# A DeltaNet recurrence feeding a hard-swish MLP on one core: the keys' transposes behind the products with the state, two steps with joined runs of small matmuls, and one last store per queue

## The chip, the cores and the metric

The kernel runs on one core of one Trainium2 chip. The metric is the device time of one execution in microseconds (us). Engines by the profile's names: PE is TensorE's matmuls, PEld its weight loads, DVE VectorE, ACT ScalarE, POOL GpSimd, SP SyncE, which only issues DMAs.

## The reference

The first half is a linear recurrence with a state matrix for each of 4 batches and 8 heads, over 768 tokens with head dimension 48. The second half is an MLP over the 3072 tokens by 384 features that the first half gives.

```
k_n = k / (norm(k) + 1e-6)
for t in range(768):                        # per batch and head
    y[t]  = q[t] @ state                    # 48 x 48 state, 0 at the start
    v_old = state^T k_n[t]
    state = state + beta[t] * outer(k_n[t], v[t] - v_old)
x   = y as (3072, 384)
h   = x @ w_in                              # 384 x 2048
g   = h * clip(h + 3, 0, 6) / 6
out = g @ w_out                             # 2048 x 384
```

All data are float32.

## The kernel before

**Chunks.** The tokens are cut into 24 steps of 32. In one step the 128 partitions hold 4 batches of 32 tokens. The recurrence inside a chunk becomes matrix products: a triangular matrix of the keys' scores per batch and head is inverted, and the state moves on once per step.

**What a step t issues.** `chain(t)` (L776) is the step's own serial work: `ks` (L795), 32 small matmuls of keys and queries with the state; `R` on DVE; `pz` (L816), 32 small matmuls with the inverse; `py` (also L816) with the scores; `su` (L927), the state's update; and `yt` (L862), three transposes of the output, which ACT copies to `xT` (L866), the input of the MLP. `prep(t)` (L494) prepares step t + 6 in five pieces: `kb` on POOL (the keys scaled, L499); four transposes of the keys on TensorE (L513), their copy by ACT (L521) and the mask on POOL (L475); the same transposes for the queries; `sc` (L536), 32 small matmuls that give the scores; and two DVE operations that mask the scores (L547), with the scaled keys on POOL (L487).

**The filler.** The MLP is cut into units that a generator (`mlp_units`, L1286) hands out one at a time between those pieces. Two steps make one block of 256 tokens. For blocks from the third on, the up projection (`up_by_eleven`, L1048) works with 11 products of 128 x 128 in place of 12, and the down projection (`down_by_seven`, L1196) with 7 in place of 8. In the trace up-projection matmuls are `ph` and down-projection ones `po`. From step 8 on, even steps are mostly filled with `ph` units, odd ones with `po` units.

**Small tiles and the full array.** `ks`, `pz`, `py`, `su` and `sc` place each matmul on a part of TensorE's array (`tile_position` or 64 rows), several side by side; a run of 32 shows as 64 loads and 64 matmuls in the trace. `ph`, `po` and the transposes use the full 128 x 128 array.

**The order of work** is written by hand: `ORDER` (L22), a list of words, for steps 0 to 4, and from step 5 on the loop at L1458. There a step has 15 slots `u`. In each slot `plan[u]` issues pieces of `chain` (`ch`) and `prep` (`now`), then one MLP unit follows. `later`, in slot 13, is the first piece (`kb`) of the prep that the next step will go on with. Step 5 (`behind`) has a plan of its own. From step 6 on, the slots around the change are:

```
0: ks            1: R, keys' transposes      2: R, queries' transposes
4: pz, scores    5: masks on the scores      (steps 8 and 12, APART: scores in 6, masks in 7)
```

Every engine works through its own queue in that order. PSUM buffers of the ring `pm` (four) are chosen when the program is written: the one whose last reader was issued first.

**Stores.** Each step's 128 x 384 output is stored by `to_dram` (L1136), one DMA for each batch of 32 rows. `py` leaves the batches in swapped order (`b ^ 1`), which `to_dram` undoes. All stores go out on SP, except that for the last two steps every second one goes out on ACT. The last block's first step is stored in two halves of 192 columns, so the end of the kernel has three stores of four DMAs.

Of the kernel before, what the change touches and what calls it, by code (L numbers as in the profile page):

```python
# [14 lines left out]
ACTF = mybir.ActivationFunctionType  # L15
# [29 lines left out]
def kernel(  # L45
# [21 lines left out]
    nc = tc.nc  # L67
    B, H, S, D = q.shape
    DM, FF = moe_w_in.shape
    C, DP = 32, 64  # L70
    P = B * C
    assert P == 128 and S % C == 0 and D <= DP and H % 2 == 0
    N = S // C
# [6 lines left out]
    CB = 2  # L80
# [14 lines left out]
    def rows(b):  # L95
        return slice(C * b, C * b + C)
# [4 lines left out]
    def group(t):  # L101
        return (0, t) if t < G0 else ((t - G0) // GS + 1, (t - G0) % GS)
# [34 lines left out]
    def needs(*what):  # L137
        assert past.issuperset(what), (what, set(what) - past)
# [5 lines left out]
    def ring(tag, n, key):  # L144

        held = rings.setdefault(tag, [])
        i = len(held)
        if i < n:
            held.append(key)
        else:  # L150
            i = min(range(n), key=lambda i: reads.get(held[i], len(reads)))
            needs(("read", held[i]))
            held[i] = key
        slot[tag] = f"{tag}{i}"

    def read(*keys):
        for key in keys:
            past.add(("read", key))
            reads.setdefault(key, len(reads))
# [49 lines left out]
    for j, value in enumerate((1.0, -1.0)):  # L209
        m = mask2[:, j, :]  # L210
        for b in range(B):
            nc.gpsimd.memset(mask2[rows(b), j, :], value)
            nc.gpsimd.affine_select(
                out=mask2[rows(b), j, :], in_=mask2[rows(b), j, :], pattern=[[1, C]],
# [89 lines left out]
    for i, n in enumerate((0, 1, 2, 3, 4, 5, 0, 1, 3, 4, 5, 0, 1, 5, 0, 1)):  # L304
        s, f = weights[i][0].shape[1:]
# [458 lines left out]
    xTs, outs, zs = {}, {}, {}  # L764
# [5 lines left out]
    def he(h):  # L770
        return (h % 2) * NP + h // 2

    def by_pair(t):
        return t.rearrange("p (a e w) -> p e a w", e=2, w=D)

    def chain(t, whole=True):  # L776
# [29 lines left out]
        def plus(out, ph, sign, into):  # L806
            for e in range(2):
                nc.vector.scalar_tensor_tensor(
                    out=by_pair(out)[:, e], in0=ph[:, e], scalar=sign, in1=by_pair(into)[:, e],
                    op0=ALU.mult, op1=ALU.add,  # L810
                )
# [14 lines left out]
        def output(Z=None):  # L826

            if t > 0:
                needs(("turned", t - 1))
            y = work.tile([P, DM], FP32, name="y", bufs=1)  # L830
            if t > 0:
                nc.scalar.activation(
                    out=by_pair(y[:]), in_=even, func=ACTF.Copy, scale=parity[:, 1, 1:2]
                )
                past.add(("even", t))
                if ("R", t) in past:
                    read(("ks", t, 0))
                yield 1
                plus(y[:], odd, parity[:, 0, 1:2], y[:])
                read(*(("ks", t, i) for i in range(2)))  # L840
                yield
            needs(("Z", t))
            Z = zs.pop(t)
            ring("pm", NPM, ("py", t))
            py = psM.tile([P, 512], FP32, name="py", tag=slot["pm"])
            of_heads(py, lambda b: b ^ 1, lambda h: LB[:, he(h), :], Z)
            past.add(("BZ", t))
            yield
            if t == 0:
                nc.scalar.activation(out=y[:], in_=py[:, 0:DM], func=ACTF.Copy)  # L850
            else:
                nc.vector.tensor_tensor(out=y[:], in0=y[:], in1=py[:, 0:DM], op=ALU.add)
            read(("py", t))
            yield
            blk, cc = divmod(t, CB)
            if cc == 0:
                needs(*([("up", blk - 2)] if blk >= 2 else []))
                xTs[blk] = work.tile([128, NKT, TB], FP32, name="xT")
            ring("pm", NPM, ("yt", t))
            pt = psM.tile([128, NKT, P], FP32, name="yt", tag=slot["pm"])  # L860
            for s in range(NKT):
                nc.tensor.transpose(pt[:, s, :], y[:, s * 128 : (s + 1) * 128], ident[:])  # L862
            past.add(("turned", t))
            yield 1
            read(("yt", t))
            nc.scalar.activation(  # L866
                out=xTs[blk][:, :, cc * P : (cc + 1) * P], in_=pt[:], func=ACTF.Copy
            )
            past.add(("seam", t))
            yield  # L870

# [11 lines left out]
        else:  # L883
# [5 lines left out]
            for e in range(2):  # L889
                nc.vector.scalar_tensor_tensor(  # L890
                    out=Rp[:, e].rearrange("p (a w) -> p a w", w=D), in0=even[:, e],
# [4 lines left out]
            if whole:  # L896
                yield
            nc.vector.scalar_tensor_tensor(
                out=Rp, in0=odd.rearrange("p e a w -> p e (a w)"), scalar=parity[:, 1, 0:1],
# [43 lines left out]
        for i, x in enumerate(su):  # L943
            sv = state[:, 2 * i : 2 * i + 2].rearrange("p b a w -> p b (a w)")
            nc.vector.tensor_tensor(
                out=sv, in0=sv, in1=x[:, :, 0 : NP * D], op=ALU.subtract
# [187 lines left out]
                yield  # L1134

    def to_dram(t, o, m=slice(0, DM)):  # L1136
        for b in range(B):
            r0 = b * S + t * C
            eng = nc.scalar if t >= N - CB and b % 2 else nc.sync
            eng.dma_start(out=out[r0 : r0 + C, m], in_=o[rows(b ^ 1), m])  # L1140

    def down(blk, c, f0):

# [186 lines left out]
    def take(gen, n=1):  # L1330
        for _ in range(n):
            while next(gen, None) == 1:
                pass
# [107 lines left out]
    with tc.manual_schedule():  # L1441
        for word in ORDER.split():
            word, _, n = word.partition("*")
            for _ in range(int(n or 1)):
                do(word)
        for name in relus:
            settle(0, name)
        while evicts:
            evicts.pop(0)()

        units = gens["u"]
        fill = inverse_of(2)
        loads = iter(())
        left = due = 0
        USED = {"up": 0.42, "eleven": 1.0, "down": 0.7}
        APART = (8, 12)
        CHAIN = {0: 0.45, 1: 0.75, 2: 0.75, 3: 0.4, 4: 0.4, 6: 0.5, 9: 0.8, 10: 0.6, 14: 0.2}
        for t in range(LS, N):  # L1458
            g, i = group(t)
            ch = chain_of(t)  # L1460
            behind = t == LS
            now, more, third, later = (prep_of(t + LA - n) for n in (2, 1, 0, -1))
            if not behind:
                now = third
            take(gens["v"], 4)
            if i == 0:
                left += 1
            if i == 2:
                loads = keys_of(g + 3)
            plan = {  # L1470
                0: lambda: take(ch),
                1: lambda: (take(ch), take(now)),
                2: lambda: (take(ch), take(now), take(gens["q"], 4)),
                3: lambda: take(ch),
                4: lambda: (take(ch), take(now, t not in APART)),
                5: lambda: take(now, t not in APART),
                6: lambda: take(now),
                7: lambda: take(now, t in APART),
                8: lambda: take(ch),
                9: lambda: take(ch),  # L1480
                10: lambda: take(ch),
                11: lambda: token_sums(t // CB),
                13: lambda: take(later),
            }
            if behind:
                plan[13] = None
                for u, gen in zip((3, 5, 5, 6, 7, 9, 10, 11, 12, 13), (more,) * 5 + (third,) * 5):
                    plan[u] = lambda old=plan.get(u), gen=gen: (old and old(), take(gen))
            ready = (1, 6)
            for u in range(NU):  # L1490
                if plan.get(u):
                    plan[u]()
                take(loads, 2)
                if (i, u) == (0, 2):
                    drain(fill)
                    left = 0
                    fill = norms_of(g + 2)
                if (i, u) == ready:
                    drain(fill)
                    fill = inverse_of(g + 1)  # L1500
                    take(fill)
                    left, due = 2 * (C - 2) + 2, 0.0
                take(rest)
                take(gens["a"])
                take(units)
                settle(1)
                while evicts:
                    evicts.pop(0)()
                if i == 1 == ready[0] and 5 < u < 7:
                    continue  # L1510
                if i == 0 or not left:
                    take(fill, 2 if i or u < 2 else u > 4)
                    continue
                room = max(1.65 - USED[mode["of"]] - CHAIN.get(u, 0), 0.15) / mode["mean"]
                due += room * left / max((GS - i) * NU - u, 1)
                due = min(due, 2.6)
                take(fill, int(due))
                left, due = max(left - int(due), 0), due - int(due)
            if behind:
                take(later)  # L1520
            drain(ch)
        for _ in units:
            settle(2)
# [30 lines left out]
```

## Time and profile before

| | us |
|---|---|
| median of 3 runs (662.1 to 663.01) | 662.82 |
| the profiled execution | 662.71 |
| its span, first to last instruction | 661.0 |

The span is what the profile covers; the profiled execution's own time is 1.7 us longer. The busy shares, the lengths of single steps and the timelines are shown where the prediction uses them. A timeline row reads: start and length in us, engine, line, operation, output from inputs, shapes, count, and in brackets the idle time before it with what ended it. Starts follow each other more closely than the lengths say, since matmuls are pipelined; a run's pace is read from start to start. A float32 matmul shows as two loads and two matmuls, a transpose as one of each. A row of the windows reads: window, its length, then busy time and count of each engine, clock, share and rate of the DMA. Of the DMA queues, q8 carries TensorE's instructions.

### The profile page before, as it was taken

The numbers are of one execution on the slowest core, as the hardware profiler recorded it, in microseconds if no ns is written. First come the engines' busy times: TensorE is split into PE (matmuls) and PEld (weight loads), VectorE is DVE, ScalarE is ACT, GpSimd is POOL, SyncE is SP. The second block draws the span as 40 slices with busy tenths as digits, with TensorE's granted clock in tenths as the row PEclk, the third lists the DMA queues.
The fourth block names the chain that finished last, engine by engine and source line by source line (L and its number), as shares of the span: only waits on it lengthen the run. The fifth ranks groups of instructions, "written<-read, shape, count | busy, mean of one in ns | idle before, by whom it ended". The sixth has DMA issues, their size and how long they took to land.

```text
span 661.0 us, 26631 instructions
## 1 busy us (share of the span) xinstructions
PE 632.6 (96%) x11640; PEld 568.8 (86%) x11640; DVE 499.5 (76%) x1164; ACT 263.2 (40%) x547; POOL 226.6 (34%) x352
## 2 busy tenths in 40 slices
PE   2768999999999999999999999999999999999997
PEld 2658987776689989999999999999999999999997
DVE  5899877798657988758988748979658998456354
ACT  4786578322232154154144244244244144153240
POOL 5531023003661354453254354164152241331330
PEclk9979999999999999999999999999999999999999
DMA  7888246212041030041030030030020020000101
GB/s 171 210 216 217 76 100 165 49 25 39 16 84 20 2 75 3 3 83 28 3 74 3 2 74 3 2 63 2 3 50 2 2 49 3 23 18 2 26 1 24
DMA packets 88692, 33.28 MB, mean 50 GB/s; under 512 B 80224, under 2 KB 83424, under 8 KB 88576
## 3 DMA queue, kind: packets, MB, share of 16 engines
q1 hardware_dynamic: 88224, 31.29, 21.5%
q8 instruction: 91, 1.49, 0.9%
q10 hardware_dynamic: 352, 0.30, 0.2%
q14 instruction: 25, 0.20, 0.1%
HBM read 26.84 MB, written 4.72 MB: 48 GB/s over the span
## 4 chain that ended last, share of the span: by engine, by line
PE 91%; DVE 3%; DMA 2%; ACT 2%; SPq 1%; issue 1%; ACTq 0%; DVEq 0%
PE po L1215 28%; PE ph L1055 27%; PE ph L983 9%; PE po L1151 6%; PE ks L795 4%; PE pz L816 3%; PE pt L513 3%; PE py L816 3%; PE su L927 3%; PE sc L536 3%; ACT spare L345 1%; PE yt L862 1%; DMA w_out<-in_moe_w_in_dram 1%; SPq L168 1%; PE pi L673 1%
## 5 line engine op out<-in xcount | busy, mean ns | idle before, releaser
L1055 PE MATMUL ph<-xT,w_in 128*128 128x128 f32 (+1 forms) x720 | 156.7, 321 | 0.2 <-issue 0.2
L1019 POOL TENSOR_TENSOR g<-g 128x256 f32<-128x256 f32 (+1 forms) x144 | 88.0, 612 | 105.5 <-ACT g L1069 99.9
L1055 PEld LDWEIGHTS ph<-xT,w_in 128*128 128x128 f32 x720 | 116.9, 191 | 6.7
L1215 PE MATMUL po<-w_out,g 128*128 128x192 f32 x640 | 110.6, 326 | 0.0
L1215 PEld LDWEIGHTS po<-w_out,g 128*128 128x128 f32 x640 | 104.6, 190 | 0.5
L1215 PE MATMUL po<-spare,g 128*128 128x192 f32 x480 | 86.7, 332 | 0.0
L1069 ACT ACTIVATE g<-ph 128x512 f32<-128x512 f32 x72 | 43.0, 597 | 107.5 <-PE ph L1055 107.5
L1215 PEld LDWEIGHTS po<-spare,g 128*128 128x128 f32 x480 | 77.2, 190 | 1.8
L983 PE MATMUL ph<-xT,w_in 128*128 128x128 f32 (+1 forms) x384 | 72.8, 339 | 1.5 <-ACT xT L866 0.6
L1225 POOL TENSOR_TENSOR o<-o,u 128x192 f32<-128x192 f32 x18 | 14.9, 828 | 163.5 <-ACT o L1222 76.1
L983 PEld LDWEIGHTS ph<-xT,w_in 128*128 128x128 f32 x384 | 60.2, 196 | 9.0 <-DVE g L993 0.9
L1082 DVE TENSOR_TENSOR g<-ph,g 128x256 f32<-128x256 f32 x72 | 30.2, 419 | 47.3 <-PE ph L1055 44.8
L748 DVE TENSOR_TENSOR pr<-A 128x30 f32<-128x30 f32 (+9 forms) x150 | 57.6, 384 | 3.3
L1201 DVE TENSOR_TENSOR g<-g 128x512 f32<-128x512 f32 x80 | 55.3, 712 | 3.6 <-PE po L1215 3.6
L1102 DVE SCALAR_TENSOR_TENSOR g<-o,g 128x512 f32<-128x512 f32 x72 | 52.5, 729 | 7.2 <-ACT o L1099 7.2
L753 DVE TENSOR_TENSOR A<-A,pr 128x30 f32<-128x30 f32 (+9 forms) x150 | 55.1, 367 | 3.3
L1055 PE MATMUL ph<-beta_tok,sums_in 128*128 128x128 f32 x288 | 55.9, 275 | 0.1
L1099 ACT ACTIVATE o<-g 128x512 f32<-128x512 f32 x72 | 45.4, 631 | 12.0 <-DVE g L1102 8.5
L345 ACT ACTIVATE spare<-spare 128x768 uint16<-128x768 uint16 (+1 forms) x56 | 47.3, 850 | 3.2 <-DMA kf<-in_k_dram 1.7
L499 POOL TENSOR_TENSOR kb<-kf,inv 128x384 f32<-128x384 f32 x24 | 21.7, 906 | 75.5 <-issue 42.6
L1222 ACT ACTIVATE o<-po 128x192 f32<-128x192 f32 x40 | 13.2, 330 | 83.2 <-PE po L1215 83.2
L1151 PE MATMUL po<-w_out,g 128*128 128x384 f32 x128 | 45.4, 490 | 0.0
(137 smaller groups left out, 1010.2 us busy)
## 6 DMA issues: line engine op xcount, KB each, us to landing
kf<-in_k_dram SPq DMA_DIRECT2D x96, 48.0 KB, 3.0
qb<-in_q_dram SPq DMA_DIRECT2D x96, 48.0 KB, 2.6
vf<-in_v_dram SPq DMA_DIRECT2D x96, 48.0 KB, 2.5
out_dram<-o SPq DMA_DIRECT2D x90, 48.0 KB, 1.6
spare<-in_moe_w_in_dram SPq DMA_DIRECT2D x4, 768.0 KB, 5.3
w_out<-in_moe_w_in_dram SPq DMA_DIRECT2D x4, 768.0 KB, 5.6
w_out<-in_moe_w_out_dram SPq DMA_DIRECT2D x4, 768.0 KB, 7.0
spare<-in_moe_w_out_dram SPq DMA_DIRECT2D x4, 768.0 KB, 4.9
```

Of the source, the lines that this page charges most:

```text
L345: nc.scalar.activation(out=z, in_=z if n else d.bitcast(I16)[:, :, :, 3], func=func, bias=value, scale=scale,)
L748: nc.vector.tensor_tensor(out=pv, in0=A[:, j + 1 :, j].unsqueeze(2).to_broadcast([n, w, j]), in1=A[:, j, 0:j].unsqueeze(1).to_broadcast([n ...
L753: nc.vector.tensor_tensor(out=A[:, j + 1 :, 0:j], in0=A[:, j + 1 :, 0:j], in1=pv, op=ALU.subtract)
L983: nc.tensor.matmul(ph[:, cols], lhsT=w_in[:, s, f * 128 : (f + 1) * 128], rhs=xT[:, s, cols], start=(s == 0), stop=(s == NKT - 1),)
L1019: nc.gpsimd.tensor_tensor(out=out, in0=a, in1=b, op=op)
L1055: nc.tensor.matmul(ph[:, n], lhsT=w, rhs=x, start=start, stop=stop, skip_group_check=True)
L1069: nc.scalar.activation(out=gt, in_=ph[:], func=ACTF.Copy)
L1099: nc.scalar.activation(out=r, in_=g, func=ACTF.Relu, bias=0.5, scale=1.0 / 6.0)
L1102: nc.vector.scalar_tensor_tensor(out=g, in0=r, scalar=1.0, in1=g, op0=ALU.min, op1=ALU.mult)
L1151: nc.tensor.matmul(pos[c][:], lhsT=gs[blk, f // 2][:, f % 2, c * P : (c + 1) * P], rhs=w_out[:, f, :], start=(f == 0), stop=(f == NFC - 1),)
L1201: nc.vector.tensor_tensor(out=A(f, *out, 4), in0=A(f, *a, 4), in1=A(f, *b, 4), op=op)
L1215: nc.tensor.matmul(ps[n][:], lhsT=A(f - f % 2, *a)[:, f % 2], rhs=b[:, f], start=(f == 0), stop=(f == HF - 1),)
```

## The change

Three edits.

1. From step 6 on, the first of the prep pieces, the keys' transposes with their copy and mask, is issued in slot 0 right behind `ks`, in place of slot 1, where a unit of the MLP lay between.
2. The list `APART` goes: in steps 8 and 12 the scores are issued in slot 4 behind `pz`, and the masks in slot 5, as in the other steps.
3. For the last block (steps 22 and 23) the copy of `yt` to `xT` becomes two copies, which put the batches back into their natural order. So two batches, 64 rows, go out in one DMA: each of the last three stores is one DMA on SP and one on ACT, in place of two and two.

```diff
@@ output() in chain()
-            nc.scalar.activation(
-                out=xTs[blk][:, :, cc * P : (cc + 1) * P], in_=pt[:], func=ACTF.Copy
-            )
+            xt = xTs[blk][:, :, cc * P : (cc + 1) * P]
+            if blk + 1 < N // CB:
+                nc.scalar.activation(out=xt, in_=pt[:], func=ACTF.Copy)
+            else:
+                xt, src = (x.rearrange("p s (i j c) -> j p s i c", j=2, c=C) for x in (xt, pt[:]))
+                for j in range(2):
+                    nc.scalar.activation(out=xt[j], in_=src[1 - j], func=ACTF.Copy)
@@ to_dram()
+        if t >= N - CB:
+            by_batch = out.rearrange("(b s) m -> b s m", s=S)[:, t * C : (t + 1) * C, m]
+            half = B // 2
+            for i, eng in enumerate((nc.sync, nc.scalar)):
+                eng.dma_start(
+                    out=by_batch[i * half : (i + 1) * half],
+                    in_=o[i * half * C : (i + 1) * half * C, m],
+                )
+            return
         for b in range(B):
             r0 = b * S + t * C
-            eng = nc.scalar if t >= N - CB and b % 2 else nc.sync
-            eng.dma_start(out=out[r0 : r0 + C, m], in_=o[rows(b ^ 1), m])
+            nc.sync.dma_start(out=out[r0 : r0 + C, m], in_=o[rows(b ^ 1), m])
@@ the plan of a step
-        APART = (8, 12)
...
-                4: lambda: (take(ch), take(now, t not in APART)),
-                5: lambda: take(now, t not in APART),
+                4: lambda: (take(ch), take(now)),
+                5: lambda: take(now),
                 6: lambda: take(now),
-                7: lambda: take(now, t in APART),
+                7: None,
...
+            if not behind:
+                plan.update({
+                    0: lambda: (take(ch), take(now)),
+                    1: lambda: take(ch),
+                })
```

The matmuls and their number stay the same. On TensorE the order changes in steps 6 to 17 alone.

## The prediction

> **What bounds the kernel now.** I read the page's busy shares first, then the chain of work that ended last, then the length of each step, then the timeline of TensorE alone.
>
> ```profile
> PE 632.6 (96%) x11640; PEld 568.8 (86%) x11640; DVE 499.5 (76%) x1164; ACT 263.2 (40%) x547; POOL 226.6 (34%) x352
> PE 91%; DVE 3%; DMA 2%; ACT 2%; SPq 1%; issue 1%; ACTq 0%; DVEq 0%
> q8 instruction: 91, 1.49, 0.9%
> ```
>
> TensorE is busy for 96% of the span and makes 91% of the chain. So an edit is worth what it takes out of TensorE's own sequence, plus what it takes from the stretch after the last matmul. The third line, one queue's row, matters below: 91 packets bring the instructions of TensorE, and 23,280 loads and matmuls over 91 packets are 256 to a packet.
>
> I cut the trace at the starts of `ks` (L795), one window per step. These are the even steps 8, 10, 12, 14 and 16, whose filler is the up projection (columns: window, its length, busy time of PE, PEld, DVE, ACT, POOL, clock, DMA):
>
> ```profile
> 233.88:258.87 24.99, 24.99 (x469) 22.78 (x471) 21.30 (x51) 11.98 (x26) 14.46 (x22) 1.00 0.23 44
> 283.96:308.76 24.80, 24.80 (x470) 22.86 (x472) 18.11 (x41) 11.98 (x26) 13.69 (x22) 1.00 0.36 64
> 333.85:358.85 25.00, 25.00 (x469) 22.79 (x472) 21.41 (x51) 11.98 (x26) 14.51 (x22) 1.00 0.22 41
> 383.94:408.88 24.94, 24.76 (x469) 22.94 (x472) 18.10 (x41) 12.10 (x26) 13.89 (x23) 1.00 0.22 40
> 433.97:459.30 25.33, 25.24 (x469) 22.86 (x473) 21.98 (x51) 12.02 (x26) 14.58 (x22) 1.00 0.20 38
> ```
>
> Steps 8 and 12 have `pz` and `sc` apart, 10, 14 and 16 have them joined already. This is the table from which the join is priced, and it also shows that joined steps are not all alike: 24.80, 24.94, 25.33.
>
> **The keys' transposes behind `ks`** (12 steps, 6 to 17). Nothing is added or removed; four transposes move ahead of one unit of products. What can change is the price of going from small tiles to the full array. An odd step of before, then the one place of the hand-written order where transposes already stand behind `ks`:
>
> ```profile
> 259.88 1.57 PE L1215 MATMUL po<-spare,g 128*128 128x192 f32 x8
> 261.29 0.60 PE L513 MATMUL pt<-ident,kb 128*128 128x128 f32 x4
> 261.72 1.47 PE L1215 MATMUL po<-spare,g 128*128 128x192 f32 x8
> 263.03 0.60 PE L513 MATMUL pt<-ident,qb 128*128 128x128 f32 x4
> ...
> 116.67 1.15 PE L795 MATMUL ks<-state,KQ 64*64 64x48 f32 x64
> 117.75 0.66 PE L513 MATMUL pt<-ident,kb 128*128 128x128 f32 x4
> 118.24 0.60 PE L513 MATMUL pt<-ident,qb 128*128 128x128 f32 x4
> ```
>
> The same eight passes take 261.29 - 259.88 = 1.41 us right behind `ks` and 263.03 - 261.72 = 1.31 us behind transposes: 0.10 for the change. Four transposes take 0.43 between products (261.72 - 261.29), 0.49 behind `ks` (118.24 - 117.75): 0.06, say 0.05, for the change. Products behind transposes pay nothing. So each step gains 0.10 - 0.05 = 0.05, 12 steps **0.6 us**. Bounds: 0 (the transposes pay 0.10 as well) to 1.2 (they pay nothing).
>
> [...]
>
> What the move brings with it: the transposes then wait for `kb` from POOL earlier. The end of `ks` and of `kb` in steps 8 and 10:
>
> ```profile
> 233.57 0.98 POOL L499 TENSOR_TENSOR kb<-kf,inv 128x384 f32<-128x384 f32 x1
> 234.88 0.49 PE L1055 MATMUL ph<-xT,w_in 128*128 128x128 f32 x2
> 283.40 0.83 POOL L499 TENSOR_TENSOR kb<-kf,inv 128x384 f32<-128x384 f32 x1
> ```
>
> `kb` ends at 234.55 and 284.23. The instruction behind `ks` starts at 234.88 in step 8, 1.00 after the step's start; in step 10 that is 284.96. It leaves 0.33 and 0.73 us, and nothing on POOL moves ahead of `kb`. If `kb` were late, every product queued behind it would wait. On ACT the copy of the keys' transposes now stands ahead of the copy of the next unit's products, on POOL the mask (two operations) ahead of that unit's sums; the products they serve are closed two units, some 4 us, later, so both cost nothing. The PSUM buffers that the transposes now take were last read a unit or more earlier.
>
> **The join in steps 8 and 12.** One entry into and one exit from small tiles go: 24.99 and 25.00 against 24.80 in step 10 give 0.2 a step, **0.4 us**. The two DVE operations on the scores come one unit earlier on DVE, into a stretch where it waited for the products anyway; step 16 has that order already.
>
> But a joined run has a price of its own, visible in steps 14 and 16:
>
> ```profile
> 398.34 0.88 PE L816 MATMUL py<-R,LB 32*32 32x48 f32 x64
> 399.40 0.38 PE L1055 MATMUL ph<-xT,w_in 128*128 128x128 f32 x2 [0.18 <-issue]
> GB/s 0 546 0 0 0 0 0 0 0 0 0 0 0 0 0 0 0 0 0 0 0 0 0 0 0 0 0 0 0 0 0 0 0 0 0 0 0 0 0 0
> q8 instruction: 1, 0.02, 5.5%
> ...
> 440.90 0.88 PE L816 MATMUL pz<-R,X 32*32 32x48 f32 x64
> 441.71 0.86 PE L536 MATMUL sc<-KQ 64*32 64x64 f32 x64
> 443.63 0.19 PEld L1055 LDWEIGHTS ph<-beta_tok,sums_in 128*128 128x128 f32 x1 [0.28 <-issue]
> GB/s 122 462 63 99 131 90 73 118 99 140 149 109 95 63 68 113 108 131 163 104 73 99 82 54 86 72 68 72 36 68 90 104 131 127 127 91 46 14 5 9
> q8 instruction: 1, 0.02, 5.6%
> ```
>
> The GB/s rows belong to windows 396.9 to 398.1 and 440.6 to 442.3, 40 slices each; the tall slice, the second in both, is the instruction packet: it starts at about 396.95 and 440.66. Its share of 16 engines gives its length: 5.5% x 16 x 1.2 = 1.06 us and 5.6% x 16 x 1.7 = 1.52, so it ends at 398.0 and 442.2. In both places TensorE stops with nothing to wait for ("issue") and goes on 1.4 us after the packet's end, at 399.40 and 443.63. Both stand where two runs of 64 loads and 64 matmuls follow each other: 256 instructions gone in 1.6 us, a whole packet, faster than the next one comes. Step 8 of before:
>
> ```profile
> 240.81 0.88 PE L816 MATMUL pz<-R,X 32*32 32x48 f32 x64
> 241.62 0.49 PE L1055 MATMUL ph<-xT,w_in 128*128 128x128 f32 x2
> GB/s 71 28 14 610 35 56 77 112 147 126 105 133 189 140 147 77 112 63 35 84 84 70 70 63 28 56 119 91 91 112 119 119 147 140 140 63 70 77 63 35
> q8 instruction: 1, 0.02, 5.3%
> ```
>
> Window 241.1 to 242.2, fourth slice: a packet starts at 241.2, takes 5.3% x 16 x 1.1 = 0.93 and is usable at 242.13 + 1.4 = 243.5. So a packet's edge lies at the start of `pz`, and its 256 instructions are `pz`, a unit, and most of `sc`; apart, they last beyond 244. Joined, they are `pz` and `sc` alone, and are used up at 241.62 + 0.80 = 242.4. The gap is up to 243.5 - 242.4 = 1.1 us; if the edge lies more than some 20 loads or matmuls further on (0.056 us each in the next unit) it is 0. I take **0.8 lost**, near the upper end, because the listing of the changed order puts the edge within the first few instructions of `pz`. Counted the same way, the edge of step 12 falls inside `sc`: no gap.
>
> The changed order also needs fewer separate wait instructions in front of the transposes: 12 fewer by step 16, 9 by step 14. The edge in step 16 so moves 12 instructions, 0.67 us, into the unit, and its gap of 0.28 closes: **0.3 gained** (0 to 0.53, the whole excess of step 16 over step 10). In step 14 both ends of the packet move alike: 0 (0.2 either way).
>
> **The end.** Each of the last three stores has two DMAs per queue before, one after. Behind the last DVE operation:
>
> ```profile
> 657.95 0.32 SPq L1140 DMA_DIRECT2D out_dram<-o  x1
> 658.31 0.48 SPq L1140 DMA_DIRECT2D out_dram<-o  x1
> 658.37 0.43 ACTq L1140 DMA_DIRECT2D out_dram<-o  x1
> ...
> out_dram<-o SPq DMA_DIRECT2D x4, 24.0 KB, 1.5
> ...
> out_dram<-o SPq DMA_DIRECT2D x90, 48.0 KB, 1.6
> ...
> kf<-in_k_dram SPq DMA_DIRECT2D x96, 48.0 KB, 3.0
> ```
>
> The last DMA starts at 658.37 and lands 1.5 later, 659.87. One DMA of 48 KB issued at 657.95 lands 1.6 later, 659.55: **0.3 gained**. Bounds: 0.42 (the whole second issue) down to a loss of 1.1 (it takes the 3.0 of the 256-row load); its 64 rows are far nearer the 32-row store. The price is on ACT: for the last two blocks of tokens, one copy of 0.49 us becomes two of half the size.
>
> ```profile
> 617.29 0.49 ACT L866 ACTIVATE xT<-yt 128x384 f32<-128x384 f32 x1 [3.61 <-PE yt L862]
> 619.46 0.28 DVE L1045 TENSOR_TENSOR beta_tok<-xT,beta_tok 128x128 f32<-128x128 f32 x1
> 620.14 0.28 PE L1055 MATMUL ph<-xT,w_in 128*128 128x128 f32 x1
> ```
>
> Two copies end at most 0.49 later than one, were each as long as the whole. Of the four DVE sums behind them the fourth starts at 619.46, so the third, which feeds the matmul at 620.14, is done 0.6 before it: that cover makes the term 0. Without cover it would be 0.49 at most.
>
> **The sum** against the profiled execution of 662.71 us (span 661.0 and 1.7 around it; the median of the runs is 662.82): - 0.6 - 0.4 + 0.8 - 0.3 - 0.3 = - 0.8, so **661.9 us**, 0.12% less. A measurement of this kernel can tell about 0.2%, 1.33 us, from no change: faster begins below 661.38, slower above 664.04.
>
> **Rivals.**
>
> *No instruction gap.* The packet for step 8 comes in time, and those of 14 and 16 do too. For it: step 10 is joined and has no gap, and neither have the odd steps. Against: the counting above. Time: 0.6 + 0.4 + 0.3, and the excess of steps 14 and 16, 0.14 + 0.53, are 2.0 us: 660.7. [...]
>
> *The transposes gain nothing.* They pay the full 0.10 behind `ks`, and the rest goes as forecast: 662.5. Against: 0.05 at 117.75, a single place.
>
> *`kb` comes late*, the slower side. In steps 8 to 16, even, POOL gives `kb` x us later than now, and TensorE stands behind `ks`. The cost is 3 (x - 0.33) + 2 (x - 0.73), the margin of step 8 for 12 and 16 and that of step 10 for 14; with the - 0.8 of the rest the kernel is slower than before from x = 0.66, and by 0.2% from x = 0.92. A mask pair of about 1.2 us ahead of `kb` would do it: 2.6 + 0.9 = 3.5 more, 665.4. Against: the mask is issued behind `kb`, in the same unit as the transposes.
>
> **How the numbers follow.** Forecast 0.53, no gap 0.30, no gain in the transposes 0.10, `kb` late 0.07. Faster by over 0.2%: the second case and a tenth of the first, 0.35. Slower: 0.07. Within: 0.58. The unknown costs of the forecast (gap 0 to 1.1, transposes 0 to 1.2, step 16 0 to 0.53, store) reach from 660.7 to 662.8; the range is 660.6 to 662.9, which leaves out the slow case and little else.
>
> **What would show it.** Right: in odd steps `ks` to `pz` 0.05 shorter; the transposes behind `ks` 0.49 long; step 12 near 24.75; step 8 with an "issue" idle of about 0.8 behind `sc` and some 25.5 long; step 16 without one; the last DMAs issued at one time per queue. Wrong: step 8 near 24.75; transposes of 0.43 or 0.55; a wait of TensorE for POOL behind `ks`; a last landing later after its issue than 1.8 us.

## The result, and the profile after

| | before | after |
|---|---|---|
| median of 7 runs, us | 662.10 (660.83 to 665.27) | 668.93 (665.41 to 669.75) |
| ratio | | 1.0079 (95%: 1.0057 to 1.0101) |
| profiled execution, span, us | 662.71, 661.0 | 665.93, 664.0 |

The changed kernel is 0.8% slower, by the ratio in the table; the two medians lie further apart, by 6.83 us. The forecast was 661.9, with 660.6 to 662.9 as its range; the time lies far outside it.

The page of the changed kernel, its busy shares and the chain that ended last:

```profile
PE 630.8 (95%) x11640; PEld 567.3 (85%) x11640; DVE 501.9 (76%) x1164; ACT 264.5 (40%) x549; POOL 227.3 (34%) x352
PE 90%; DVE 3%; DMA 2%; SPq 1%; issue 1%; ACT 1%; DVEq 0%
```

TensorE is busy 1.8 us less than before (630.8 against 632.6), and the span is 3.0 longer. So the time was not lost among the products. Divided into stretches, by the starts of `ks` and of the last matmul, the two profiled executions compare like this:

| stretch, us | before | after | difference |
|---|---|---|---|
| up to `ks` of step 6 | 183.17 | 181.18 | -1.99 |
| steps 6 to 17 | 301.14 | 300.30 | -0.84 |
| steps 18 to 22 | 116.25 | 116.25 | 0 |
| step 23 up to the last matmul | 56.64 | 56.64 | 0 |
| last matmul to the end of the span | 3.80 | 9.63 | **+5.83** |
| span | 661.0 | 664.0 | +3.0 |

A span is given to 0.1 us, so the last stretch holds to 0.05, here and in the runs below. The first stretch has the same instructions in both. In the twelve traces of this study it ends between 181.18 and 185.17, whatever the kernel, so I put its -1.99 down to chance; it hid two fifths of the loss. Without it the loss is 5.83 - 0.84 = 5.0 us, 0.75% of 662.7, close to the ratio's 0.79%. The medians show 1.8 us more than that. The spread of the first stretch is wide enough for it, but that it lies there is not shown, since one execution of the seven was traced.

**The steps.** The windows of the changed kernel from `ks` to `ks`, steps 8, 10, 12, 14 and 16, with the columns of the prediction's table:

```profile
231.71:256.92 25.21, 25.14 (x466) 22.82 (x466) 22.16 (x52) 12.23 (x26) 14.84 (x22) 1.00 0.24 44
281.96:306.71 24.75, 24.75 (x466) 22.82 (x465) 18.05 (x41) 12.23 (x26) 13.79 (x22) 1.00 0.36 64
331.75:356.68 24.93, 24.93 (x467) 22.75 (x466) 22.28 (x52) 12.22 (x26) 14.93 (x22) 1.00 0.22 41
381.72:406.47 24.75, 24.75 (x466) 22.82 (x465) 18.04 (x41) 12.23 (x26) 13.99 (x23) 1.00 0.23 42
431.51:456.44 24.93, 24.93 (x467) 22.74 (x466) 22.27 (x52) 12.23 (x26) 14.93 (x22) 1.00 0.19 36
```

Step 10 is 0.05 shorter than before, step 14 0.19, step 16 0.40, step 12 only 0.07, and step 8 is 0.22 longer.

**The end.** The timeline of the changed kernel for the last stores, SP and ACT:

```profile
654.03 0.53 SPq L1145 DMA_DIRECT2D out_dram<-o  x1
654.03 0.52 ACTq L1145 DMA_DIRECT2D out_dram<-o  x1
...
655.11 0.51 SPq L1145 DMA_DIRECT2D out_dram<-o  x1
655.12 0.52 ACTq L1145 DMA_DIRECT2D out_dram<-o  x1
```

One DMA per queue and store, as the change says, and the last one is issued right behind the last DVE operation (654.73 + 0.35). But the span ends at 664.0, 8.9 us after that issue. The DMA view of the last stores, first of the kernel before, in its window 656.8 to 661.0 (40 slices of 0.105 us; busy tenths of the 16 engines, rate, packets):

```profile
DMA  0000000049768988923582026730000000000000
GB/s 0 0 0 0 0 0 0 0 117 249 191 161 190 278 176 205 234 74 59 132 213 66 0 51 161 161 96 0 0 0 0 0 0 0 0 0 0 0 0 0
DMA packets 384, 0.30 MB, mean 70 GB/s; under 512 B 128, under 2 KB 384, under 8 KB 384
```

then of the changed kernel, 653.9 to 664.0 (slices of 0.2525 us):

```profile
DMA  0000011010101101111111111111111111000000
GB/s 0 0 0 0 0 24 18 12 12 18 30 36 36 36 12 49 55 55 49 49 43 52 46 49 55 43 49 52 46 43 49 46 46 37 21 3 0 0 0 0
DMA packets 264, 0.29 MB, mean 29 GB/s; under 512 B 8, under 2 KB 264, under 8 KB 264
```

The same 256 packets of data (384 - 128 and 264 - 8), the same 288 KB. Before, they drain in 2.0 us (slices 8 to 26) at up to 278 GB/s; after, in 7.8 us (slices 5 to 35), never over 55 GB/s, with about a tenth of the 16 engines busy. In the traces a packet of data is one row of 1536 or 768 bytes, a small packet 4 bytes. The small packets hint at why the drain is slow: 128 over 8 DMAs are 16 per DMA, 8 over 4 DMAs are 2 per DMA. They stand behind the data of their DMA. I read them as one per DMA engine that took part (the "completion packets" of the expectations below): 16 engines before, **2** after. What they carry is not shown. The packets' own times agree with the counts: more than ten are under way at once for 1.2 of the 2.0 us before, two for 6.3 of the 7.6 us (first packet to last) after. What sets the 2 is to be shown. The diff offers a candidate: the DRAM side of the new DMA is 2 batches of 32 rows, where that of the old one was 32 rows.

### The profile page after: what moved, and what is told of

It is laid out like the page before. It is cut to its first block, busy times and chain, and to the rows that moved or that the text cites. A ratio compares the mean times of both kernels' runs of the same rounds, so it can differ in the third digit from the quotient of the medians.

```text
span 664.0 us, 26610 instructions
## 1 busy us (share of the span) xinstructions
PE 630.8 (95%) x11640; PEld 567.3 (85%) x11640; DVE 501.9 (76%) x1164; ACT 264.5 (40%) x549; POOL 227.3 (34%) x352
## 4 chain that ended last, share of the span: by engine, by line
PE 90%; DVE 3%; DMA 2%; SPq 1%; issue 1%; ACT 1%; DVEq 0%
PE po L1227 28%; PE ph L1059 27%; PE ph L987 9%; PE po L1163 6%; PE ks L795 4%; PE pt L513 3%; PE su L931 3%; PE pz L816 3%; PE py L816 3%; PE sc L536 2%; PE yt L862 1%; DMA w_out<-in_moe_w_in_dram 1%; SPq L168 1%; PE pi L673 1%; DMA kf<-in_k_dram 1%
## 5 line engine op out<-in xcount | busy, mean ns | idle before, releaser
L1059 PE MATMUL ph<-xT,w_in 128*128 128x128 f32 (+1 forms) x720 | 156.0, 320 | 0.1
L1227 PE MATMUL po<-spare,g 128*128 128x192 f32 x480 | 85.1, 331 | 0.0
L987 PE MATMUL ph<-xT,w_in 128*128 128x128 f32 (+1 forms) x384 | 71.0, 333 | 2.4 <-DVE g L997 1.8
L1237 POOL TENSOR_TENSOR o<-o,u 128x192 f32<-128x192 f32 x18 | 13.4, 745 | 163.2 <-ACT o L1234 75.6
L748 DVE TENSOR_TENSOR pr<-A 128x30 f32<-128x30 f32 (+9 forms) x150 | 59.0, 393 | 3.3
```

What stands on the lines that cost most here:

```text
L748: nc.vector.tensor_tensor(out=pv, in0=A[:, j + 1 :, j].unsqueeze(2).to_broadcast([n, w, j]), in1=A[:, j, 0:j].unsqueeze(1).to_broadcast([n ...
L987: nc.tensor.matmul(ph[:, cols], lhsT=w_in[:, s, f * 128 : (f + 1) * 128], rhs=xT[:, s, cols], start=(s == 0), stop=(s == NKT - 1),)
L1059: nc.tensor.matmul(ph[:, n], lhsT=w, rhs=x, start=start, stop=stop, skip_group_check=True)
L1227: nc.tensor.matmul(ps[n][:], lhsT=A(f - f % 2, *a)[:, f % 2], rhs=b[:, f], start=(f == 0), stop=(f == HF - 1),)
```

## The experiments

**Theory: two engines.** The candidate, to be tested: the number of DMA engines follows the outermost dimension of the access pattern, and `[2][32][192]` puts everything on 2. **Rivals:** the steps lose (the joins, the transposes); the two ACT copies delay the last block; a DMA of 64 rows is slow by its size alone. The diffs are excerpts, and stand against the changed kernel where nothing else is said.

### The first two edits alone (steps_only)

```diff
-                for j in range(2):
-                    nc.scalar.activation(out=xt[j], in_=src[1 - j], func=ACTF.Copy)
...
+            nc.scalar.activation(
+                out=xTs[blk][:, :, cc * P : (cc + 1) * P], in_=pt[:], func=ACTF.Copy
+            )
...
+            eng = nc.scalar if t >= N - CB and b % 2 else nc.sync
+            eng.dma_start(out=out[r0 : r0 + C, m], in_=o[rows(b ^ 1), m])
```

> The first two edits alone; copies and stores as before. Theory (two engines): all that was lost lies in the last stores, whose DMAs show two completion packets each in the trace of the changed kernel where those of before show sixteen, so without them the kernel gains what its steps 6 to 17 gained, about 0.8 us: 0.8 below the kernel before, with 3.4 us from the last DVE operation to the end of the span. Rival (the steps lose): with the joins or the transposes behind the loss, it is 5 us above the kernel before.

Measured: 661.62 us median, ratio 0.9998 (0.9984 to 1.0012); 3.73 from the last matmul to the end; steps 6 to 17 last 300.61. The loss is gone, so the steps do not lose. The gain expected was too high: the trace shows 0.5 in the steps, since step 8 is longer here (25.51) than in the changed kernel (25.21), and the runs can't tell it from none.

### The third edit alone (stores_only)

```diff
-                4: lambda: (take(ch), take(now)),
+                4: lambda: (take(ch), take(now, t not in APART)),
...
-                7: None,
+                7: lambda: take(now, t in APART),
...
-                0: lambda: (take(ch), take(now)),
```

> The third edit alone: two copies to xT, and one DMA of 64 rows per queue for each of the last three stores. Theory (two engines): 5.8 us above the kernel before (9.3 us from the last DVE operation to the end, in place of 3.4), steps 6 to 17 as before. Rival (the steps lose): within 0.5 us of the kernel before.

Measured: 667.86, ratio 1.0099 (1.0078 to 1.0119), 6.5 us; 9.68 from the last matmul to the end; steps 6 to 17 last 300.92. The third edit alone makes the loss.

### The two copies, but four DMAs (four_stores)

```diff
-                eng.dma_start(
-                    out=by_batch[i * half : (i + 1) * half],
-                    in_=o[i * half * C : (i + 1) * half * C, m],
-                )
...
+            last = t >= N - CB
+            eng = nc.scalar if last and b >= B // 2 else nc.sync
+            eng.dma_start(out=out[r0 : r0 + C, m], in_=o[rows(b if last else b ^ 1), m])
```

> The changed kernel with its two copies and the natural order of the batches, but each store again as two DMAs of 32 rows per queue. Theory (two engines): sixteen completion packets per DMA and 3.4 us from the last DVE operation to the end; 0.8 us below the kernel before. Rival (the copies): the loss comes from the two copies with their strided reads, which delay the last block; then it stays some 5 us above the kernel before.

Measured: 662.89, ratio 1.0004 (0.9988 to 1.002); 3.73 from the last matmul to the end, and the stretches from step 18 to the last matmul at 116.25 and 56.64 as in all others. The copies cost nothing; it is the DMAs.

### The same 64 rows in another order (token_first)

```diff
-                xt, src = (x.rearrange("p s (i j c) -> j p s i c", j=2, c=C) for x in (xt, pt[:]))
+                xt = xt.rearrange("p s (c i j) -> j p s i c", i=2, j=2)
+                src = pt[:].rearrange("p s (i j c) -> j p s i c", j=2, c=C)
-            by_batch = out.rearrange("(b s) m -> b s m", s=S)[:, t * C : (t + 1) * C, m]
+            by_token = out.rearrange("(b s) m -> s b m", s=S)[t * C : (t + 1) * C, :, m]
-            half = B // 2
+            half = C // 2
```

SP stores the first 16 tokens of all four batches, ACT the other 16.

> The changed kernel with the last block's rows in token order (32 tokens of 4 batches in place of 4 batches of 32 tokens), so that one DMA per queue has an outermost dimension of 16 tokens, each with 4 rows; the same 64 rows and bytes per DMA. Theory (two engines: the number of DMA engines follows the outermost dimension, 2 in the changed kernel): sixteen completion packets per DMA, some 3.1 us from the last DVE operation to the end, and 1.1 us below the kernel before. Rival (size: a DMA of 64 rows in separate pieces lands late whatever its order): 9 us from the last DVE operation to the end, 5 above the kernel before.

Measured: 662.38, ratio 1.0004 (0.999 to 1.0018), 3.77 from the last matmul to the end. The DMA view of its last two stores, window 655.0 to 659.2:

```profile
DMA  0000000000003589893300265473000000000000
DMA packets 320, 0.30 MB, mean 70 GB/s; under 512 B 64, under 2 KB 320, under 8 KB 320
...
out_dram<-o SPq DMA_DIRECT2D x1, 96.0 KB, 2.2
out_dram<-o ACTq DMA_DIRECT2D x1, 96.0 KB
out_dram<-o SPq DMA_DIRECT2D x1, 48.0 KB
out_dram<-o ACTq DMA_DIRECT2D x1, 48.0 KB, 2.1
```

64 small packets over 4 DMAs are 16 each, and the drain is 1.7 us (slices 12 to 27 of 0.105). The number of rows, of bytes and of DMAs is that of the changed kernel; the order of the dimensions differs, and with it which 64 rows go together. The rival of size falls. But the gain that was forecast for one DMA in place of two does not come either: 3.77 against 3.80 before. The DMA of 64 rows takes 0.55 us to issue and lands 2.1 after its issue, against 0.32 to 0.48 and about 1.5 for 32 rows, which eats the saved second issue.

### Four and eight (one_of_four, eight_first)

The first on top of the changed kernel, the second on top of token_first:

```diff
-            for i, eng in enumerate((nc.sync, nc.scalar)):
...
+            nc.sync.dma_start(out=by_batch, in_=o[:, m])
```

```diff
-            half = C // 2
-            for i, eng in enumerate((nc.sync, nc.scalar)):
+            half = C // 4
+            for i, eng in enumerate((nc.sync, nc.sync, nc.scalar, nc.scalar)):
```

> The changed kernel with one DMA of all 128 rows for each of the last three stores, on SP alone: four batches of 32 rows, so an outermost dimension of 4 in place of 2, and twice the bytes per DMA. Theory (the number of engines is the outermost dimension): four completion packets per DMA, and the data drain about twice as fast, so from the last matmul to the end some 6 us (5.5 to 7) in place of 9.6. Rival (size: more rows and bytes per DMA land later): 9.6 or more. Both: above the kernel before, where that stretch is 3.8.

> The kernel with the last rows in token order, but two DMAs of 32 rows per queue with an outermost dimension of 8 tokens, as many rows and bytes per DMA as in the kernel before, whose outermost dimension is 32 rows. Theory (the number of engines follows the outermost dimension): eight completion packets per DMA, and a drain of the last 288 KB between those on 4 engines (4.1 us) and 16 (1.6 to 2.0), near 2.4; last matmul to the end 4.0 to 4.7. Rival (only DMAs of more than 32 rows are slow): sixteen packets, a drain of 2.0 and 3.8 to the end.

Measured: one_of_four 665.35, ratio 1.0047 (1.0031 to 1.0062), 6.19 from the last matmul to the end; eight_first 664.41 in one execution, 4.99. The DMA view of one_of_four's last two stores, 657.0 to 665.2, slices of 0.205:

```profile
DMA  0000000000000023221122222232222221000000
GB/s 0 0 0 0 0 0 0 0 0 0 0 0 0 7 45 37 15 15 37 45 60 97 90 105 82 90 120 86 94 90 94 94 82 53 0 0 0 0 0 0
DMA packets 264, 0.29 MB, mean 36 GB/s; under 512 B 8, under 2 KB 264, under 8 KB 264
```

and of eight_first's, 657.0 to 662.6, slices of 0.14:

```profile
DMA  0000000000044440442421403104022000000000
DMA packets 320, 0.30 MB, mean 53 GB/s; under 512 B 64, under 2 KB 320, under 8 KB 320
```

8 small packets over 2 DMAs are 4 each, 64 over 8 are 8 each. The drains are 4.3 us (slices 13 to 33) and 2.8 (11 to 30). So for an outermost dimension of 2, 4, 8 and 16 the same 288 KB take 7.8, 4.3, 2.8 and 1.7 us (to within a slice), and the stretch to the end 9.63, 6.19, 4.99 and 3.77. The biggest DMA of all (one_of_four) is faster than that of the changed kernel, and the one of 32 rows in groups of 8 slower than the 32 rows of before (2.0): neither fits a price by size. eight_first came out 0.3 above what was expected of it.

### Both DMAs on one queue (sp_alone)

```diff
-            for i, eng in enumerate((nc.sync, nc.scalar)):
+            for i, eng in enumerate((nc.sync, nc.sync)):
```

> The changed kernel with both DMAs of each of the last three stores on SP, one behind the other, still 2 batches of 32 rows each. Theory (the two queues share the same two DMA engines): the 288 KB of the last two stores drain as slowly as from two queues, 7.6 us, and the last matmul to the end takes 9.6 to 10.3 (the later issue at most). Rival (two engines per queue, four in all): half the engines, some 13 us from the last matmul to the end.

Measured in one execution: 666.32, and 9.61 from the last matmul to the end, against 9.63. The DMA view of its last two stores, 654.4 to 664.5:

```profile
GB/s 0 0 0 0 0 24 18 18 12 24 36 24 43 24 49 24 55 49 49 49 24 43 49 49 61 49 40 46 49 43 49 49 43 49 30 0 0 0 0 0
...
q1 hardware_dynamic: 264, 0.29, 9.7%
```

One queue alone reaches the same 49 GB/s as two. The two queues of the changed kernel do not have two engines each; by these counts they share the two. The packets' own times in the traces agree: two packets are under way at once for 6.6 of the drain's 7.5 us here, as for 6.3 of 7.6 in the changed kernel. In one_of_four, whose packets take 12.5% of 16 engines in its view of 8.2 us, the mean over the drain of 4.3 us is 12.5% x 16 x 8.2 / 4.3 = 3.8. So the last store, 48 KB per queue, also stood behind the 192 KB of the store issued 1.1 us before it.

So the small packets per DMA were 2, 4, 8 and 16 with 2 against 64, 4 against 128, 8 against 32 and 16 against 64 (DRAM rows or batches against partitions), and 16 with the 32 rows of before. The busy tenths of the 16 engines in the views above peak in the same order: at 1 in the changed kernel, 3 in one_of_four, 4 in eight_first, and 9 in token_first and before. Only the DRAM side was ever the small one in these runs, so what a small number of partitions does is not shown. The traces do not number the engines; that both queues use the same ones is read from sp_alone, where one queue takes 9.61 us to the end and two take 9.63.

### Which part of the steps' gain is whose (transposes_only, join_12)

```diff
+                4: lambda: (take(ch), take(now, t not in (8, 12))),
+                5: lambda: take(now, t not in (8, 12)),
...
+                7: lambda: take(now, t in (8, 12)),
```

Both on top of steps_only; this is transposes_only, and join_12 has `(8,)` in place of `(8, 12)`.

> The first edit alone: keys' transposes behind the products with the state, scores of steps 8 and 12 apart, copies and stores as before. Theory (the joins are worth nothing): odd steps 25.04, steps 8 and 12 near 24.95, step 16 near 24.93, so steps 6 to 17 last 300.1 us, 0.9 less than in the kernel before (301.0) and 0.4 less than with the joins (300.6). Rival (as forecast, a join is worth 0.2 where no gap follows): step 12 near 24.95 here and 24.75 in the kernel that joins step 12 alone.

> The first edit and the join of step 12, step 8 left apart; copies and stores as before. Theory (the join is worth nothing in step 12, since another wait stands there): step 12 at 24.93, within 0.05 of the kernel with the first edit alone. Rival (worth 0.2): step 12 at 24.75.

Measured: transposes_only 662.11, ratio 0.999 (0.9975 to 1.0006), steps 6 to 17 in 300.06; join_12 661.49, ratio 0.9989 (0.9976 to 1.0003), 300.05. Windows of steps 8, 12 and 16 in transposes_only:

```profile
234.61:259.56 24.95, 24.95 (x466) 22.74 (x465) 21.60 (x52) 12.21 (x26) 14.81 (x22) 1.00 0.23 44
334.39:359.34 24.95, 24.95 (x466) 22.74 (x465) 21.71 (x52) 12.21 (x26) 14.88 (x22) 1.00 0.21 41
434.17:459.10 24.93, 24.93 (x466) 22.74 (x465) 22.28 (x52) 12.21 (x26) 14.95 (x22) 1.00 0.19 38
```

and of step 12 in join_12:

```profile
332.20:357.12 24.92, 24.92 (x466) 22.73 (x465) 22.26 (x52) 12.10 (x26) 14.93 (x22) 1.00 0.21 41
```

The join is worth 0.03 in step 12 (24.95 to 24.92), not 0.2. Its waits say where the rest stays; those of TensorE's loads in the changed kernel, steps 6 to 17:

```profile
PEld yt L862 <- ACT o L1103: 0.7, 2, 0.4
```

Two of the twelve steps, 12 and 16, have it (before, step 16 alone): the transposes of `yt` come earlier by the join and then stand for ACT. The product ahead of them starts 17.55 into step 12 in join_12 and 17.76 in transposes_only, so up to there the join does save 0.2. The first transpose then starts 0.36 later in join_12 and 0.22 in transposes_only: 0.14 of the 0.2 goes there.

The prediction priced the join by step 10. Its own table shows another kinship: steps 8, 12 and 16 have 51 operations on DVE, 10 and 14 have 41. Joined and without a gap, step 12 comes out as step 16 does (24.93 both), not as step 10 (24.75). That the ten more operations are what makes ACT late is not shown.

These two kernels have the shortest steps, 1.0 us below before in the trace, and nothing lost at the end. They are the versions to prefer, but their intervals still reach 1: 1.0 us is 0.15%, under what these runs can tell.

### The instruction packet moved (edge_moved)

```diff
-            for p in range(NP):
+            for p in [*range(NP)] * (4 if (t, j) == (12, 0) else 1):
                 nc.tensor.transpose(
```

on top of steps_only.

> The first two edits, stores as before, and the keys' transposes of step 6 issued four times over into the same place (the last of them counts), which adds 24 instructions to TensorE two steps ahead of the gap in step 8. Theory (instruction packets of 256): step 6 longer by 12 transposes at 0.11, to 26.8; the edge of the packet moves 24 instructions ahead, into the unit before pz, so 1.3 us more pass before the packet is used up, and the gap behind sc in step 8 (0.33 to 0.79 in four traces) goes: step 8 at 24.75. Rival (the gap comes from the join itself, a drain of small tiles or a PSUM buffer): step 8 stays at 25.2 to 25.7.

Measured in one execution: 664.10, span 662.4. Windows of steps 6, 8 and 16:

```profile
183.95:210.76 26.81, 26.81 (x439) 23.58 (x438) 18.73 (x44) 7.97 (x19) 12.26 (x17) 1.00 0.33 60
235.80:260.67 24.87, 24.87 (x466) 22.74 (x466) 22.16 (x52) 12.21 (x26) 14.83 (x22) 1.00 0.23 45
435.33:460.66 25.33, 25.19 (x466) 22.81 (x465) 22.27 (x52) 12.21 (x26) 14.92 (x22) 1.00 0.18 37
```

The instruction packet of TensorE in step 8, first in steps_only, window 242.0 to 244.0, then here, window 239.0 to 241.0, 40 slices of 0.05 each; the tall slices are the eighth and the thirteenth:

```profile
GB/s 134 96 146 150 108 73 42 385 38 27 127 111 81 108 111 115 131 85 54 88 142 192 207 139 62 4 0 0 0 0 0 0 4 4 8 8 12 4 12 8
q8 instruction: 1, 0.02, 4.0%
...
GB/s 27 65 131 154 131 123 108 85 62 96 77 69 458 131 161 127 54 8 31 27 12 65 81 61 62 100 127 134 142 135 146 208 177 234 169 108 46 12 8 12
q8 instruction: 1, 0.02, 2.9%
```

In steps_only the packet starts at 242.4, 0.3 ahead of `pz`, and takes 4.0% x 16 x 2.0 = 1.3, to 243.7; TensorE goes on 1.4 later, at 245.0. Here it starts at 239.6, 3.1 ahead of `pz`. The gap in step 8 is gone, with pz and sc joined as they were, and a gap is back in step 16 where steps_only has none (24.93). So 24 instructions in step 6, two and ten steps ahead, decide it: a join has a gap or none by the place of the packet's edge. Step 8 at 24.87, not 24.75, has a wait at `yt` as well, 0.31 from the product ahead to the first transpose.

## Why the prediction was wrong, point by point

- **The end: this step failed.** The term for the stores put a DMA's cost by the wrong thing. The price "One DMA of 48 KB issued at 657.95 lands 1.6 later", with a loss of 1.1 as its worst bound, was read by rows and bytes ("far nearer the 32-row store"). What counted in these runs is the outermost dimension: 2 batches, 2 small packets per DMA, so by that reading 2 engines, which both queues and two stores share. Forecast -0.3, measured **+5.83**. The rows that served as bounds, a store of 32 rows and a load of 256, have no dimension of 2 and so said nothing of it. The small packets (16 per DMA before) were in the view and not read. The sign named for it, a last landing later than 1.8 us after its issue, came: the last packets end at 662.8 (in slice 35 of the view above), 7.7 after the issue at 655.11. With 16 small packets per DMA the term is 0.0 (token_first, 3.77 to the end against 3.80), so even then the -0.3 was not there.
- **The range** did not take in the bounds of its own terms. With no gain in the transposes and in step 16, the gap at 1.1 and the store's loss of 1.1, the sum is 664.5, not 662.8; at the other ends it is 660.2, not 660.7. Even 664.5 lies under every execution of the changed kernel (from 665.41), so these bounds, rightly added, would not have held the time either: the store's was too small.
- **The transposes: right,** mechanism and size. -0.05 in each step, -0.6 in all: odd steps 25.09 to 25.04, steps 8 and 12 25.00 to 24.95 (transposes_only), step 10 24.80 to 24.75. The transposes behind `ks` take 0.50 in the changed kernel (from 207.75 to the next product at 208.25), against 0.49 forecast.
- **The joins: the mechanism right, the size off.** -0.4 forecast, and step 12 "near 24.75" as a sign. Step 12 gave 0.03 and stands at 24.93, and step 8 without a gap gave 0.08 (24.95 to 24.87), so -0.1: a later wait took most of the rest.
- **The gap in step 8: right.** 0.8 forecast. The matmuls behind sc in steps_only:

```profile
243.48 0.86 PE L536 MATMUL sc<-KQ 64*32 64x64 f32 x64
244.27 0.38 PE L1055 MATMUL ph<-xT,w_in 128*128 128x128 f32 x1
245.01 0.38 PE L1055 MATMUL ph<-xT,w_in 128*128 128x128 f32 x1 [0.37 <-issue]
```

  From one product to the next 0.74 where 0.11 is the pace: 0.63 lost (shown as 0.37 idle, since a matmul's modelled end covers the rest). Over the seven traces with the join in step 8 and stores of any kind the step is 25.21 to 25.93, mean 25.56, so against 24.87 without a gap it costs 0.3 to 1.1, on average 0.7.
- **Step 16: right.** -0.3 forecast, 25.33 and 25.27 (before, stores_only) to 24.93, of which 0.05 are the transposes'. The packet came no earlier: it ends 8.29 into step 16 before and 8.40 after, so what its instructions cover has moved, as forecast; that it moved by 12 is counted, not shown. Step 14, put at 0, is 24.80 in stores_only with the order of before, so its -0.19 is mostly that of one trace.
- **The copies: right,** 0.
- **Sum of the steps:** -0.5 forecast without the end; -0.84 in the profiled execution, -0.53 in steps_only. That the latter meets the forecast is in part luck: the joins gave 0.3 less, and step 14 and a smaller gap gave as much. The rival "no instruction gap" fell by step 8, "the transposes gain nothing" by the odd steps, "`kb` late" by the even ones, where TensorE never waits for POOL. (That rival's own threshold was off: a cost of 0.8 is reached at x = 0.60, not 0.66, since step 10's margin adds nothing below 0.73.) The loss came by none of them; a store of which the trace showed no example had been given no rival.

## What to carry to other kernels

Before two DMAs are merged into one, look at the outermost dimension, and at the small packets per DMA in the trace of a DMA of that very shape: here a merge that left 2 there had 2 small packets per DMA in place of 16, and its last 288 KB took 7.8 us in place of 2.0. Where rows of several batches go out together, try the longer dimension outside, with the rows put in that order on the way: 16 tokens outside brought the drain to 1.7 (token_first). A price by the nearest row of the trace holds only if the row agrees in what sets the price; where it does not, the range has to reach further.

## What the runs showed of the hardware that was not expected

- The drain per engine is about 22 to 25 GB/s with packets of 768 and 1536 bytes. This is an estimate, worked out from 49 GB/s with 2 small packets per DMA (changed kernel) and some 90 with 4 (one_of_four), one engine for each.
- SP's and ACT's DMAs with an outermost dimension of 2 drain no faster from two queues than from one: 9.63 us from the last matmul to the end against 9.61, at 49 GB/s both. I read that as shared engines.
- One DMA of 64 rows with 16 small packets is no better at the end than two of 32: 2.1 us against about 1.5 to land, 0.55 against 0.32 to 0.48 to issue.
- The start, up to step 6, varies by 4 us between executions of the same instructions (181.18 to 185.17), nearly four times the 1.1 us that the best order of the steps gave (transposes_only, join_12).
